# Sixty 64-column zero matmuls in place of two 512-column ones ahead of a two-layer convolution and MLP kernel

## The chip, the cores and the metric

The kernel runs on one core of a Trainium2 chip. The metric is the device time in microseconds of one execution, as the median of several runs; lower is better. The engines are called PE or TensorE (matmuls; PEld is its weight load), DVE or VectorE, ACT or ScalarE, POOL or GpSimd, and SP, which here only issues transfers.

## The reference

Two layers, each made of a gated long convolution (A) and an MLP (B), with the same weights in both layers. The sequence has 2048 positions, the width is 512 and the MLP's inner width 1376.

```
def _A_ref(q, k, v, shift_k, ssm_k, ssm_D):        # S = 2048, D = 512
    k_shift = sum over t < 4 of k delayed by t, times shift_k[:, t]
    kv = k_shift * v
    y = irfft(rfft(kv padded to 2S) * rfft(ssm_k padded to 2S))[:S]   # causal long convolution
    return q * (y + kv * ssm_D)
def _B_ref(x, w1, b1, w2, b2):
    return gelu(layernorm(x) @ w1 + b1) @ w2 + b2

x = A_q
x = x + _A_ref(_layernorm(x), A_k, A_v, A_shift_k, A_ssm_k, A_ssm_D)
x = x + _B_ref(_layernorm(x), ...)
x = x + _A_ref(_layernorm(x), ...)
x = x + _B_ref(_layernorm(x), ...)
```

## The kernel before

The convolution's factor y + kv * ssm_D does not depend on x, so it is computed once and used in both layers. Everything lies in one SBUF tensor "ar" (bf16), a small one "sm" (f32) and PSUM "ps", which is handed out in pieces of two banks or one.

Operations are recorded first (`P.op`), with the memory that they read and write; then a list `ORDER`, written out in the file, gives the order of all operations on all engines, `BANKS` gives each PSUM tile its bank, and semaphore waits are worked out from the recorded dependences. Each engine runs its own operations strictly in that order. Loads are issued by SP, a few small ones by ACT, and wait for nothing.

The stages in the order in which they touch the first 65 us:

- L493 (POOL) clears a 128x512 block; L499 (PE) multiplies that block of zeros with itself eight times into the first PSUM tile ("warm"). Nobody reads the result.
- L528 (PE) transposes the filter `ssm_k` in four groups of 16 matmuls, each behind its load; L453 copies each group out (DVE). L450 on POOL and DVE adds `ssm_D` into one row of each group. L511 (PE) spreads the shift taps over all partitions.
- L545 (PE) is the first stage of the filter's transform, 16 operations of 16 matmuls; L453 (ACT or DVE) evicts each one. L558 (PE) is the second stage, 16 operations of 8 matmuls, evicted by L453 as well.
- The shift of k by up to three positions is done in two ways. For channel blocks 0 and 1 PE transposes k (L589) and multiplies it with diagonal matrices of the taps (L606); the eight matrices, 128x128 each, are made by POOL (L520) from the identity, and L613 (DVE) multiplies with v. For channel blocks 2 and 3 DVE does it with elementwise operations of 128x2048 (L450).
- Then the same transform for kv (L545), its second stage (L651), the product with the filter (L450), and two inverse stages (L674, L731), with evictions by L453.

POOL's order in this part is: memsets (L504, L493, L471), L517, two small L450 (each behind a VectorE copy of L528's results), two memsets (L489), four L520, a small memset (L710), four L520. The matrices are made for the blocks in the order 0, 1, 0, 1 and then 0, 1, 1, 0; so the first L606, which is block 1's, needs the seventh, and block 0's needs the eighth.

From about 76 us on, the layers run: layer norm statistics and updates on DVE and POOL (L754 to L768, L450), transposes, the MLP's matmuls (L827, L860), the gelu on ACT (L832) and the addition on DVE (L864).

Of the kernel before, what the change touches and what calls it, by code (L numbers as in the profile page):

```python
# [367 lines left out]
def bass_interleave_layers__ssm_conv_h3__mixer_channel_mlp__prompt_kernel(  # L368
# [7 lines left out]
    def A(p0, n, off, *dims):  # L376
        return bass.AP(ar, p0 * AR + off, [[AR, n]] + [list(d) for d in dims])
# [7 lines left out]
    def Q(tile, p0, n, off, *dims):  # L385
        return bass.AP(ps, p0 * 4096 + tile.base * 512 + off, [[4096, n]] + [list(d) for d in dims])
# [65 lines left out]
    def evac(engs, dst, src, tile):  # L452
        f = {ACT: lambda e: e.activation(dst, src(), AF.Copy), DVE: lambda e: e.tensor_copy(dst, src())}  # L453
        return P.op(engs, f, writes=[dst], tile=tile)
# [14 lines left out]
    z = A(0, 1, R_K + c0, [512, 3], [1, WDV])  # L469
# [17 lines left out]
    for i in range(NPE):  # L487
        z = A(0, 128, R_KT[i], [130, 16], [1, 2])
# [3 lines left out]
    z = A(0, 128, R_W, [1, 512])  # L492
    P.op(POOL, lambda e, z=z: e.memset(z, 0.0), writes=[z])  # L493
    P.tag = "warm"
    tl = Tile(2)

    def f(e, tl=tl, z=z):
        for i in range(8):
            r = e.matmul(Q(tl, 0, 128, 0, [1, 512]), z[:, :128], z, start=True, stop=True)  # L499
        return r  # L500
    warm = P.op(PE, f, reads=[z], tile=tl)

    one = A(0, 1, R_ONE, [1, 128])
    P.op(POOL, lambda e: e.memset(one, 1.0), writes=[one])  # L504
    P.tag = "taps"
    tl = Tile(2)
    ins = [(i, A(0, 1, R_SR + 512 * c, [1, 512])) for i, c in enumerate(DV_CH)]

    def f(e, ins=ins, tl=tl):
        for i, m in ins:  # L510
            r = e.matmul(Q(tl, 0, 128, 512 * i, [1, 512]), one, m, start=True, stop=True)  # L511
        return r
    P.op(PE, f, reads=[one] + [m for _, m in ins], tile=tl).preds[warm.i] = "psum"
    for i in range(NDV):
        evac(ACT, A(0, 128, R_SJ + i * 512, [128, 4], [1, 128]), lambda tl=tl, i=i: Q(tl, 0, 128, 512 * i, [1, 4], [4, 128]), tl)
# [6 lines left out]
    for b in range(4):  # L522
        tl = Tile(2)
# [27 lines left out]
    def stage2(G, ks, n):  # L551

        tl = Tile(2)
        ins = [(i, A(0, 128, R_S2 + k * 128, [1, 128]), A(0, 128, G + k * n, [1, n])) for i, k in enumerate(ks)]

        def f(e):
            for i, w, m in ins:
                r = e.matmul(Q(tl, 0, 128, i * n, [1, n]), w, m, start=True, stop=True)  # L558
            return r
        P.op(PE, f, reads=[x for y in ins for x in y[1:]], tile=tl)  # L560
        return tl
# [5 lines left out]
    for k8 in range(16):  # L567
        tl = stage2(R_G, range(8 * k8, 8 * k8 + 8), 128)
# [203 lines left out]
    def ntmp():  # L772
        nn[0] += 1
        return R_N + (nn[0] % 8) * 512
# [3 lines left out]
    for L in range(2):  # L778
        s0 = 0
        for n in (BLOCKS0, BLOCKS1)[L]:  # L780
# [6 lines left out]
            for i, s in enumerate(sl):  # L787
                z = ntmp()
# [12 lines left out]
            for i, s in enumerate(sl):  # L801
                z = ntmp()
# [6 lines left out]
                tl = Tile(1)  # L809
# [9 lines left out]
            for fc in range(11):  # L819
                rows = 128 if fc < 10 else 96  # L820
                tl = Tile(1)
# [13 lines left out]
            for i, s in enumerate(sl):  # L835
                P.tag = "m2"
                tl = Tile(1)
# [63 lines left out]
```

## Time and profile before

| what | value |
|---|---|
| median of 3 runs | 241.46 us (241.1 to 242.47) |
| span of the profiled execution, first to last instruction | 238.8 us (the page gives no other time of that execution) |
| PE busy | 226.2 us (95%), 2312 matmuls |
| PEld busy | 151.6 us (63%) |
| DVE busy | 171.6 us (72%) |
| ACT busy | 138.3 us (58%) |
| POOL busy | 41.3 us (17%) |
| eight warm matmuls (L499) | 1.56 to 4.9 us, 3.33 us busy |
| first filter transpose (L528) | starts at 4.78 us |

All positions are in us from the first instruction of the profiled execution. Busy time is the time in which at least one instruction of an engine is recorded as running; matmuls overlap each other, so the spacing of two starts says more than the duration of one. "issue" stands for time in which an engine waited for nothing that the profile shows. An arrow names what ended an idle time.

### The profile page before, as it was taken

Reading aid. Unit: us, or ns where it says so; the run is one execution under the profiler, and the core shown is the slowest. Engines: PE = TensorE matmul, PEld = TensorE weight load, DVE = VectorE, ACT = ScalarE, POOL = GpSimd, SP = SyncE. Lnnn points to the kernel's source line nnn. Section 1 sums busy time; section 2 is a strip of 40 time slices with the busy share of each in tenths; the row PEclk is TensorE's granted clock in tenths of the full one; section 3 lists DMA queues with packets and bytes.
Section 4 is the critical chain, followed back from the end, with each engine's and each line's share of the span. In section 5 each row is a group of like instructions: output and inputs, shape, how many; then the busy total and the mean of one; then the engine's idle time right before and its main releaser. Section 6 shows DMA issues by size and latency. Waiting matters only on the chain.

```text
span 238.8 us, 5555 instructions
## 1 busy us (share of the span) xinstructions
PE 226.2 (95%) x2312; PEld 151.6 (63%) x2332; DVE 171.6 (72%) x359; ACT 138.3 (58%) x225; POOL 41.3 (17%) x77
## 2 busy tenths in 40 slices
PE   7987989886999999999999999999999999999995
PEld 3875778875899886766766667644444444444543
DVE  0979999999999999999887999693793312030035
ACT  2598799999999995642754444342782042454100
POOL 2179000000013444041230310400220200000000
PEclk9999999999999999999999999999999999999999
DMA  6999949999960003111122022240013021310024
GB/s 241 364 342 383 383 148 253 249 272 309 379 227 0 3 0 68 26 23 31 37 47 44 0 48 44 45 88 3 0 22 66 3 44 31 101 44 3 0 71 148
DMA packets 37035, 27.40 MB, mean 115 GB/s; under 512 B 19506, under 2 KB 29969, under 8 KB 37010
## 3 DMA queue, kind: packets, MB, share of 16 engines
q1 hardware_dynamic: 36446, 26.91, 37.8%
q8 instruction: 18, 0.29, 0.5%
q10 hardware_dynamic: 564, 0.14, 0.4%
q14 instruction: 7, 0.06, 0.1%
HBM read 16.82 MB, written 2.10 MB: 79 GB/s over the span
## 4 chain that ended last, share of the span: by engine, by line
PE 77%; ACT 9%; DMA 4%; DVE 4%; SPq 3%; issue 3%; ACTq 0%
PE ps L860 31%; PE ps L827 30%; ACT ar L453 9%; PE ps L674 5%; PE ps L731 3%; SPq L439 3%; PE ps L545 3%; DMA ar<-in_A_ssm_k_dram 2%; DVE ar L453 2%; DMA ar<-ar 2%; PE ps L528 1%; PE ps L606 1%; PE ps L849 1%; DVE sm L754 1%; PE ps L589 1%
## 5 line engine op out<-in xcount | busy, mean ns | idle before, releaser
L832 ACT ACTIVATE ar<-ps,sm 128x256 bf16<-128x256 f32 (+4 forms) x143 | 64.7, 525 | 72.5 <-PE ps L827 68.1
L827 PE MATMUL ps<-ar 128*128 128x256 bf16 (+4 forms) x568 | 84.2, 297 | 0.2
L860 PE MATMUL ps<-ar 128*128 128x512 bf16 (+1 forms) x329 | 79.0, 379 | 0.6
L453 ACT ACTIVATE ar<-ps 128x1024 bf16<-128x1024 f32 (+1 forms) x81 | 72.5, 1057 | 9.0 <-PE ps L511 4.5
L827 PEld LDWEIGHTS ps<-ar 128*128 128x128 bf16 (+1 forms) x572 | 52.9, 100 | 29.8 <-ACT ar L832 0.5
L450 DVE TENSOR_TENSOR ar<-ar 128x512 bf16<-128x512 bf16 (+3 forms) x106 | 63.6, 634 | 2.0 <-DMA ar<-in_A_k_dram 1.3
L860 PEld LDWEIGHTS ps<-ar 128*128 128x128 bf16 (+1 forms) x341 | 33.1, 98 | 34.3 <-ACT ar L832 0.3
L864 DVE TENSOR_TENSOR ar<-ar,ps 128x512 bf16<-128x512 bf16 x31 | 20.6, 680 | 47.3 <-PE ps L860 47.3
L754 DVE BATCH_NORM_STATS2 sm<-ar 128x6 f32<-128x512 bf16 (+1 forms) x68 | 42.8, 647 | 0.1
L768 DVE TENSOR_SCALAR ar<-ar,sm 128x512 bf16<-128x512 bf16 x64 | 25.0, 407 | 7.8 <-POOL sm L762 5.2
L760 POOL TENSOR_SCALAR sm<-sm 128x2 f32<-128x2 f32 (+2 forms) x26 | 6.0, 232 | 93.9 <-DVE sm L756 93.3
L762 POOL TENSOR_TENSOR sm<-sm 128x2 f32<-128x2 f32 (+2 forms) x26 | 21.6, 832 | 2.2
L545 PE MATMUL ps<-ar 128*64 128x128 bf16 x512 | 17.1, 221 | 1.4 <-issue 0.8
L545 PEld LDWEIGHTS ps<-ar 128*64 128x64 bf16 x512 | 14.9, 110 | 3.2 <-issue 1.0
L674 PE MATMUL ps<-ar 128*128 128x128 bf16 x256 | 15.0, 220 | 0.6 <-ACT ar L453 0.6
L674 PEld LDWEIGHTS ps<-ar 128*128 128x128 bf16 x256 | 14.7, 114 | 0.8 <-ACT ar L453 0.8
L453 DVE CAST ar<-ps 128x1024 bf16<-128x1024 f32 x11 | 13.0, 1212 | 0.3 <-PE ps L558 0.3
L651 PE MATMUL ps<-ar 128*128 128x64 bf16 x256 | 9.8, 194 | 3.2 <-ACT ar L453 2.7
L453 DVE COPY ar<-ps 128x2048 bf16<-128x2048 bf16 (+1 forms) x8 | 8.2, 1024 | 6.4 <-PE ps L528 6.3
L651 PEld LDWEIGHTS ps<-ar 128*128 128x128 bf16 x256 | 8.2, 98 | 4.7 <-ACT ar L453 3.9
L756 DVE BATCH_NORM_AGGREGATE sm<-sm 128x2 f32<-128x6 f32 (+1 forms) x64 | 9.9, 171 | 0.3
L558 PE MATMUL ps<-ar 128*128 128x128 bf16 x128 | 8.6, 220 | 0.8 <-ACT ar L453 0.8
(34 smaller groups left out, 78.1 us busy)
## 6 DMA issues: line engine op xcount, KB each, us to landing
ar<-tab_s SPq DMA_DIRECT2D x16, 256.0 KB, 9.6
ar<-ar SPq DMA_DIRECT2D x16, 256.0 KB, 4.2
ar<-in_A_ssm_k_dram SPq DMA_DIRECT2D x4, 512.0 KB, 5.3
ar<-in_A_k_dram SPq DMA_DIRECT2D x8, 256.0 KB, 7.6
ar<-in_A_v_dram SPq DMA_DIRECT2D x8, 256.0 KB, 9.6
ar<-in_A_q_dram SPq DMA_DIRECT2D x4, 512.0 KB, 7.9
out_dram<-ar SPq DMA_DIRECT2D x7, 256.0 KB, 2.1
ar<-in_B_w_dram SPq DMA_DIRECT2D x1, 1376.0 KB, 12.6
```

What stands on the lines that cost most here:

```text
L450: return P.op(eng, lambda e: e.tensor_tensor(o, a, b, op), reads=[a, b] + list(more), writes=[o])
L453: f = {ACT: lambda e: e.activation(dst, src(), AF.Copy), DVE: lambda e: e.tensor_copy(dst, src())}
L545: r = e.matmul(Q(tl, 64 * ri, 64, i * 128, [1, 128]), w, m, start=True, stop=True)
L651: r = e.matmul(Q(tl, 0, 128, i * pitch, [1, n]), w, m, start=True, stop=True)
L674: r = e.matmul(Q(tl, 0, 128, i * 128, [1, 128]), w, m, start=q == 0, stop=q == 1)
L754: P.op(DVE, lambda e, sj=sj, x=x: e.bn_stats(sj, x), reads=[x], writes=[sj])
L762: P.op(POOL, lambda e: e.tensor_tensor(r, v, hf, ALU.pow), reads=[v, hf], writes=[r])
L768: P.op(DVE, lambda e: e.tensor_scalar(o, x, m, r, ALU.subtract, ALU.mult), reads=[x, m, r], writes=[o])
L827: r = e.matmul(Q(tl, 0, rows, 0, [1, w]), a, m, start=dk == 0, stop=dk == 3)
L832: P.op(ACT, lambda e, dst=dst, tl=tl, rows=rows, bias=bias, w=w: e.activation(dst, Q(tl, 0, rows, 0, [1, w]), AF.Gelu_apprx_tanh, bias=bia ...
L860: r = e.matmul(Q(tl, 0, 128, 0, [1, 512]), ins[fc][0], ins[fc][1], start=fc == 0, stop=fc == 10)
L864: P.op(DVE, lambda e, x=x, tl=tl: e.tensor_tensor(x, x, Q(tl, 0, 128, 0, [1, 512]), ALU.add), reads=[x], writes=[x], tile=tl)
```

## The change

In the warm operation the eight matmuls of 512 columns become six of 512 columns followed by sixty of 64 columns. All of them use the same zero block, the first 128 columns of it as weights, and write the same PSUM tile. The operation stays one operation of the list, with the same place, the same dependences and the same PSUM tile; all other operations, their order, their engines and their waits are the same in both kernels. Each matmul is issued as a weight load and a matmul, so TensorE's program grows from 16 to 132 instructions here. In the changed kernel, lines behind the change have numbers higher by two.

```
     def f(e, tl=tl, z=z):
-        for i in range(8):
+        for i in range(6):
             r = e.matmul(Q(tl, 0, 128, 0, [1, 512]), z[:, :128], z, start=True, stop=True)
+        for i in range(60):
+            r = e.matmul(Q(tl, 0, 128, 0, [1, 64]), z[:, :128], z[:, :64], start=True, stop=True)
         return r
     warm = P.op(PE, f, reads=[z], tile=tl)
```

## The prediction

> **What bounds the kernel now.** I read the chain of work that ended last first, because the change sits in the first 5 us and only what the chain carries on from there can reach the end. These are its pieces up to 26 us (start, us, what):
>
> ```profile
> 1.18 4.84 DMA ar<-in_A_ssm_k_dram
> ...
> 14.81 0.79 issue
> 15.60 1.47 PE ps L545 x45
> ...
> 20.77 1.31 issue
> 22.08 1.01 PE ps L589 x15
> ...
> 25.32 4.69 ACT ar L453 x5
> ```
>
> The filter (L528, L545) starts behind a load. Twice TensorE stands still for "issue", with no wait on anything in the program. From 25.32 on, ScalarE's evictions set the pace. The waits of ScalarE from 25.3 to 64 us hold one line only (us in total, times, longest):
>
> ```profile
> ACT ar L453 <- PE ps L558: 2.6, 1, 2.6
> ```
>
> The busy times by stretch (PE, PEld, DVE, ACT and POOL busy) say the same:
>
> ```profile
> 25.30:40.00 14.70, 13.50 (x191) 11.06 (x191) 14.55 (x13) 14.68 (x16) 0.00 (x0) 1.00 0.82 247
> 52.00:63.00 11.00, 8.70 (x191) 7.75 (x192) 11.00 (x11) 11.00 (x14) 0.00 (x0) 1.00 0.98 317
> 76.40:121.00 44.60, 44.34 (x381) 33.06 (x385) 42.85 (x132) 27.95 (x68) 15.21 (x33) 1.00 0.14 27
> ```
>
> ScalarE has no gap after 25.32 until 78 us, and from 64 us TensorE is full too (12.85 of 13.40, 44.34 of 44.60). So whatever moves ScalarE's start at 25.32 moves the end by as much. What sets that start is the first tap matmul (L606, 22.88) and the first L558 behind it (24.62). The timeline, engine by engine:
>
> ```profile
> 1.56 3.33 PE L499 MATMUL ps<-ar 128*128 128x512 bf16 x8 [1.56 <-POOL ar L493]
> 4.78 1.22 PE L528 MATMUL ps<-ar 128*128 128x128 bf16 x16
> ...
> 16.42 2.36 DVE L450 TENSOR_TENSOR ar<-ar 128x2048 bf16<-128x2048 bf16 x2 [1.28 <-DMA ar<-in_A_k_dram]
> 19.83 3.58 DVE L450 TENSOR_TENSOR ar<-ar 128x2048 bf16<-128x2048 bf16 x3
> ...
> 13.86 2.70 POOL L520 TENSOR_SCALAR ar<-ar,sm 128x128 bf16<-128x128 bf16 x4
> 16.81 7.07 POOL L520 TENSOR_SCALAR ar<-ar,sm 128x128 bf16<-128x128 bf16 x4
> ```
>
> GpSimd builds the eight diagonal tap matrices (L520). Four take 0.60 each, then 2.36, 0.60, 2.61 and 1.22: the long ones are those that overlap VectorE's L450 runs at 16.42 and 19.83. The first L606 needs the seventh of them, done at 22.57, 0.3 before it starts.
>
> **Step 1, the start of the filter.** Removed: two 512-column matmuls. The trace starts one every 0.425 us; the seventh starts at 4.094 and the full rate comes at 4.49 (the eighth takes 380 ns, the others 631). Added: sixty of 64 columns with 128x128 weights. The nearest row is L651, the same shape at the full rate: a pair of load and matmul every 29.5 ns. At the low rate no such row exists; 512 columns go from 425 to 216 ns (L860, four in 0.86), a ratio of 1.97, hence 58 ns as an estimate. (The page's PEclk row says 9 from the first slice on and does not show this; the spacing does.) From 4.094, seven run slow (0.40) and 53 at full rate (1.56): they end at 6.06, and L528 starts at 6.1 instead of 4.78, **+1.3**. Bounds: all at the full rate, 5.86, +1.1; all at the low rate, 7.57, +2.8. I take 1.3, since the six matmuls before 4.09 are unchanged. L528's load landed at 4.73, so it hides none of this; the second one's load (6.03) did hold TensorE for 0.3, and this now disappears.
>
> **Step 2, to GpSimd.** L528's results go through four VectorE copies of 1.23 (6.04, 7.34, 9.04, 11.65). The second started 0.06 late behind its load and will now follow the first at once; later ones gain a little more against L545. Adding these I get the fourth copy ending at 13.95 instead of 12.88: **+1.05 to +1.1**. GpSimd's 12.96 (L450) waits for it, and behind that, in its own queue, stand two memsets and all eight L520. So L520 starts at 14.95, not 13.86.
>
> **Step 3, the two "issue" stalls.** Between the resumptions at 15.60 and 22.08 TensorE takes 126 weight loads, 126 matmuls and 4 semaphore waits: 256 instructions. The queue "instruction" of TensorE moved 16 KB at 13.01 and 19.54, each landing 1.1 later, and TensorE went on 1.4 to 1.5 after that. So it waits for its own instructions, in blocks of 256; entering a block starts the next fetch, and 6.5 us pass from one entry (15.60) to the next (22.08). The change adds 58 pairs, 116 instructions, so both block ends move 116 instructions forward in the work: into the L545 that ran at 12.41, and into the one that ran at 18.00. The first is reached at 13.9; its block was entered about 6.1 and comes at 12.5 to 13.0, so there is no stall and TensorE regains 0.8. The second, entered about 12.9, comes at 19.4 to 19.9 and is reached at 18.6: a stall of about 1, but now in front of four L545 and not behind them. Redoing the evictions behind it (0.91 each on ScalarE), L589 ends at 22.4 (before 23.04). By TensorE alone L606 would start at 22.3, **0.6 earlier** than before. The third block would come at 26.6, needed at 28: hidden by ScalarE.
>
> **Step 4, what is late instead.** GpSimd. VectorE's run at 16.42 starts with a load of k, which the change does not touch. Before, four L520 had begun by then. At +1.1 the third begins at 16.35 and the fourth, at 17.05, falls into the run. Giving them the slots that the trace shows (one ends at 19.17, one at 19.87, one at 22.57, one at 23.88), the seventh ends at 23.88 instead of 22.57, and L606 starts at 23.93, **+1.05**. If the delay of step 2 is over 1.16, the third misses 16.42 too: the seventh then ends at 24.6 and L606 starts at 24.63, **+1.75**. These are 0.1 us apart in their cause, and I take the first, as my sum is 1.05 to 1.1. [...]
>
> **The sum.** The profiled execution has a span of 238.8; the page gives no other time of it, and the median of the three runs, 241.46, is 2.66 above (start and end around the span). 238.8 + 1.05 = 239.85, and with 2.66 **242.5**, or +0.43%. No other queue issues anything new.
>
> **Rivals.**
> - *The third tap misses the gap* (above): +1.75, 243.2. For it: a margin of 0.1 us, and the arrival of k can differ as much from run to run. Against: my sum falls short of 1.16.
> - *Not slower*: GpSimd is no gate, because L520 gets through beside VectorE after all (its durations are said to be rough), and the block ends now lie better. Then L606 starts at 22.3, L558 waits only for ScalarE's last eviction of the filter's first stage, at 24.1, and starts at 24.2 instead of 24.62: -0.4, 241.1. It decides if the seventh L520 ends before 22.3. Against: two L520 cannot take 2.4 and 2.6 of themselves where six take 0.6 or 1.2.
> [...]
> - *Another block is late*: a fetch under loads takes longer than 7 us and stalls TensorE beyond ScalarE's reserve, +1.5 to +2.5, about 243.5.
> - *The change does nothing of the kind*: that TensorE waits for the load anyway. It landed at 4.73, so no.
>
> **How the numbers follow.** A measurement of this kernel tells about 0.5% (1.21 us) from no change. Chances: +1.05, 0.42; +1.75, 0.28; not slower, 0.13; low rate, 0.10; another block, 0.07. The second, the fourth and the fifth lie beyond 1.21 us (together 0.45, of which 0.02 may fall back inside). The first is only 0.16 below that, and a third of it, 0.13, may come out above: slower 0.43 + 0.13 = 0.56. Of the not-slower case 0.04 may reach beyond -1.21: faster 0.04, and 0.40 is left for the same. The range takes the first two whole with 0.3 of scatter, the upper part of the not-slower case and most of the late block: 241.2 to 243.9; it leaves the low rate out.
>
> **What would show it.** Right: L528 starts near 6.1; no "issue" stall near 15 and one near 18.6 to 19.8, in L545; L589 ends before 23; the seventh L520 ends at 23.9 or 24.6 with two or three of them long; L606 right behind it; ScalarE idle until 26.4 or 27.1 and dense after. Wrong: if L606 starts before 22.9, or starts late although the seventh L520 is done, or if ScalarE's dense part shows gaps.

## The result, and the profile after

The changed kernel takes 242.74 us (median of 12 runs, 242.19 to 243.34) against 241.4 us for the kernel before (12 runs, 240.84 to 242.61): ratio 1.0049, 95% interval 1.0029 to 1.0070. That is 1.3 us more. The forecast was 242.5, in a range of 241.2 to 243.9, with 0.56 for "slower" and 0.40 for "the same"; the measured 0.49% lies just under the 0.5% that the prediction took as the bound between the two.

The profiled execution has a span of 240.6 us (its own time is 242.39, so 1.8 us lie around the span; over all timed executions on record it is 1.75 to 1.96). The span is 1.8 longer than the one shown of before. Its chain of work that ended last, up to 31 us (start, us, what):

```profile
1.56 2.74 PE ps L499 x6
4.30 1.90 PE ps L501 x60
6.20 2.01 PE ps L530 x32
...
18.57 1.91 issue
20.48 0.48 PE ps L547 x9
20.95 0.02 issue
20.98 3.88 ACT ar L453 x4
24.86 1.75 PE ps L608 x13
26.61 0.46 PE ps L560 x8
27.07 0.02 issue
27.09 3.77 ACT ar L453 x4
```

Line numbers are two higher here (L608 is the L606 of before, L560 the L558, L547 the L545, L591 the L589, L522 the L520, and L530 the L528, which the text calls L528 throughout). The warm matmuls now stand in the chain, where before a load stood. There is one pause for "issue" instead of two; it is longer, and it lies in front of the last evictions of the filter's first stage. ScalarE's dense part starts at 27.09 instead of 25.32, **1.77 later**. One step of the chain is not what it says: the first of L608's 14 matmuls has no record in this trace, and its time is put down as a wait for ScalarE. L608's first weight load started at 24.32, right behind those of L591, and in e9 below L608 ran ahead of the end of the same eviction (24.50 against 24.85). So L608 followed TensorE's own work here. GpSimd and TensorE in the timeline:

```profile
14.86 4.37 POOL L522 TENSOR_SCALAR ar<-ar,sm 128x128 bf16<-128x128 bf16 x4
19.49 5.15 POOL L522 TENSOR_SCALAR ar<-ar,sm 128x128 bf16<-128x128 bf16 x4
...
18.16 0.41 PE L547 MATMUL ps<-ar 128*64 128x128 bf16 x7
20.48 2.34 PE L547 MATMUL ps<-ar 128*64 128x128 bf16 x57 [1.91 <-issue]
22.75 1.89 PE L591 MATMUL ps<-ar 128*128 128x128 bf16 x16
24.85 1.38 PE L608 MATMUL ps<-ar 128*128 128x384 bf16 x9 [0.22 <-ACT ar L453]
```

Sixteen L591 take 1.89 us here; before, sixteen L589 took 1.07 (at 17.00). The windows say why: the third number from the end is the granted clock, 0.50 in one stretch.

```profile
18.10:21.60 3.50, 1.59 (x50) 1.38 (x49) 3.50 (x4) 2.27 (x3) 3.25 (x4) 1.00 1.03 380
21.60:25.00 3.40, 3.18 (x42) 2.95 (x38) 2.20 (x3) 3.25 (x4) 2.85 (x3) 0.50 1.06 382
25.00:28.00 3.00, 2.95 (x37) 2.34 (x36) 2.25 (x3) 0.91 (x1) 0.00 (x0) 1.00 1.04 381
```

(Columns: stretch, its length, busy time and count of PE, PEld, DVE, ACT and POOL, granted clock, DMA share, GB/s.) The clock was at half from 21.57 to 24.98 in this execution, from 1.1 us behind the end of the pause on.

From ScalarE's start on, nothing is gained or lost. Taking each ScalarE operation's start less its start in the execution of before, the lag is 1.77 at 25.4 us, 1.71 at 48, 1.76 at 76, 1.77 at 120, 1.77 at 220, and the spans differ by 1.77.

### The profile page after: what moved, and what is told of

The parts are those of the page before. It is cut to its first block, busy times and chain, and to the rows that moved or that the text cites. A ratio compares the mean times of both kernels' runs of the same rounds, so it can differ in the third digit from the quotient of the medians.

```text
span 240.6 us, 5671 instructions
## 1 busy us (share of the span) xinstructions
PE 228.1 (95%) x2370; PEld 154.5 (64%) x2390; DVE 171.5 (71%) x359; ACT 138.3 (57%) x225; POOL 41.1 (17%) x77
## 4 chain that ended last, share of the span: by engine, by line
PE 78%; ACT 11%; DVE 3%; issue 2%; SPq 2%; DMA 2%; POOL 0%; ACTq 0%; POOLq 0%
PE ps L862 30%; PE ps L829 30%; ACT ar L453 10%; PE ps L676 5%; PE ps L733 3%; SPq L439 2%; PE ps L547 2%; PE ps L530 2%; DMA ar<-ar 2%; DVE ar L453 1%; PE ps L608 1%; PE ps L499 1%; PE ps L851 1%; DVE sm L756 1%; PE ps L560 1%
## 5 line engine op out<-in xcount | busy, mean ns | idle before, releaser
L450 DVE TENSOR_TENSOR ar<-ar 128x512 bf16<-128x512 bf16 (+3 forms) x106 | 63.7, 635 | 1.0 <-ACT ar L453 0.5
L547 PE MATMUL ps<-ar 128*64 128x128 bf16 x512 | 17.3, 224 | 2.3 <-issue 1.9
L547 PEld LDWEIGHTS ps<-ar 128*64 128x64 bf16 x512 | 15.3, 112 | 4.0 <-issue 2.1
L560 PE MATMUL ps<-ar 128*128 128x128 bf16 x128 | 8.6, 220 | 0.8 <-ACT ar L453 0.8
```

What stands on the lines that cost most here:

```text
L450: return P.op(eng, lambda e: e.tensor_tensor(o, a, b, op), reads=[a, b] + list(more), writes=[o])
L547: r = e.matmul(Q(tl, 64 * ri, 64, i * 128, [1, 128]), w, m, start=True, stop=True)
```

## The experiments

My theory, called "gates" below: the extra time is not the sixty matmuls as such. It is set by two things that they shift, where TensorE's blocks of 256 instructions end (in the execution of before it stood still for 0.79 and 1.31 us there), and whether GpSimd's taps get in ahead of VectorE's run at about 16.4 us (0.60 us for an L520 ahead of it, 2.36 for the one beside it). The rivals are "delay alone" (the end moves with the first L528), "number of instructions" and "low clock" (the half rate of the profiled run is the cause). Every kernel was timed in turns with the kernel before on the same chip; in part of the executions of most of these kernels, the one before among them, the mean granted clock is 0.990 to 0.993 and not 1.0 (0.993 in the execution above, whose clock was at half for 3.41 us), so a time alone says little and the traces are read as well. Without the executions in which it fell (a mean granted clock below 0.997) the medians are 241.5 for the kernel before, 242.69 for e1, 244.14 for e2, 240.99 for e3, 241.05 for e4 and 243.12 for e5; the changed kernel's is 242.78.

**e1, instructions without delay.** The 104 extra instructions, with no later start.

```
-        for i in range(8):
-            r = e.matmul(Q(tl, 0, 128, 0, [1, 512]), z[:, :128], z, start=True, stop=True)
+        for i in range(60):
+            r = e.matmul(Q(tl, 0, 128, 0, [1, 64]), z[:, :128], z[:, :64], start=True, stop=True)
```

> Only the sixty 64-column matmuls, no 512-column one: 104 more instructions than before, and no later start (50 at 58 ns up to 4.49 and 10 at 29.5 ns end at 4.8, where before L528 started at 4.78). Gates (my theory: block ends of TensorE's instructions, then GpSimd's taps): the block ends fall 104 instructions earlier in the work; the first block is entered at about 7.7 and comes at about 14.2 but is needed at 13.1, the second comes at 20.7 to 21.2 and is needed at 18.5; L606 starts at 23.4 instead of 22.9 and ScalarE's dense part 0.5 to 1.0 later: +0.5 to +1.0 us on before. Delay alone (the end moves by as much as the first L528): 0. [...]

Measured: 243.52 against 241.62, ratio 1.0072 (1.0039 to 1.0104). L528 started at 5.17 in the trace (its load came late), 0.4 later than in the execution shown of before, and ScalarE's dense part at 27.59, 2.27 later. TensorE's part of it:

```profile
18.37 0.58 PE L545 MATMUL ps<-ar 128*64 128x128 bf16 x13
21.14 2.76 PE L545 MATMUL ps<-ar 128*64 128x128 bf16 x51 [2.19 <-issue]
23.83 1.53 PE L589 MATMUL ps<-ar 128*128 128x128 bf16 x16
25.20 0.98 PE L606 MATMUL ps<-ar 128*128 128x512 bf16 x6
```

Delay alone falls: it expected 0, or 0.4 with the late load of this execution. The pause sits where the block end was expected, and the seventh L520 was long done (20.84), so here TensorE's own instructions hold L606, and not the taps. The block came at 21.14, within the time that I had given it (20.7 to 21.2), but the half rate followed at 21.42 and stretched the work behind the pause. The five timed runs with no fall of the clock have a median of 242.69, some 1.2 above those of the kernel before (241.5), beyond the expectation's upper end. The span of this trace is 3.5 longer than the one of before, and not 2.27: the other 1.3 lie behind the last operation, where the last outputs landed later.

**e2, delay without instructions.** `range(8)` becomes `range(14)`, 512 columns each.

> Fourteen 512-column matmuls: L528 starts at 6.0 as in the changed kernel, with 12 more instructions instead of 116. Gates: both block stalls stay behind about the same work as before and come 1.2 later, the seventh L520 ends at 23.9, L606 starts at 24.0: +1.2 us on before, up to +1.9 if a stall of over 2 us brings the half rate. Delay alone: +1.3. Number of instructions alone (the 116 extra ones are the price, not the start): 0 to +0.2.

Measured: 244.14 against 241.62, ratio 1.0084 (1.0051 to 1.0118), +2.0 us by the ratio, and 2.6 where the clock did not fall. The same delay with 104 instructions fewer costs no less than the change (1.0084 against 1.0049, with intervals that overlap), so the number of instructions alone is not the price. L606 was held by GpSimd, as expected:

```profile
22.63 0.35 PE L545 MATMUL ps<-ar 128*64 128x128 bf16 x5 [1.35 <-issue]
22.92 1.07 PE L589 MATMUL ps<-ar 128*128 128x128 bf16 x16
24.37 1.85 PE L606 MATMUL ps<-ar 128*128 128x512 bf16 x13 [0.39 <-POOL ar L520]
```

ScalarE started 1.44 later. What I had not put in is further down: a block end near 46 us now stalls TensorE beyond ScalarE's reserve (0.74 of idle ScalarE at 47.78, TensorE idle 0.71 for "issue" at 46.94), which makes the lag 2.27, and between 90 and 95 us, where L827 waits 0.44 for a transfer, it grows to 2.89.

**e3, the changed kernel with the taps in another order.** In `ORDER`, operations 56 and 58, and 57 and 61, change places, so that GpSimd makes block 1's four matrices first. All operations are kept.

```
-  ... 91, 24, 56, 78, ... 89, 57, 87, ... 80, 61, 29, 183, 58, 199, ...
+  ... 91, 24, 58, 78, ... 89, 61, 87, ... 80, 57, 29, 183, 56, 199, ...
```

> The changed kernel with GpSimd making the four matrices of channel block 1 before those of block 0, so that the first L606 needs the fourth L520 (19.2) and not the seventh (23.9). Gates: L606 starts as soon as TensorE is there: 22.4 without the half rate, and L558 then waits for ScalarE's last eviction at 24.1 to 24.9: 0 to +0.3 us on before, 0.7 to 1.0 less than the changed kernel. Low clock as the cause in every run: L606 at 24.3 as in the profiled run of the changed kernel, no gain over it. Delay alone: no gain, +1.3 on before.

Measured: 241.01 against 241.62, ratio 0.9970 (0.9940 to 0.9999). The whole cost of the change is gone, though L528 started at 6.58 in this trace and the pause for "issue" is still there:

```profile
20.87 1.81 PE L547 MATMUL ps<-ar 128*64 128x128 bf16 x57 [1.74 <-issue]
22.61 1.07 PE L591 MATMUL ps<-ar 128*128 128x128 bf16 x16
23.52 1.91 PE L608 MATMUL ps<-ar 128*128 128x512 bf16 x14
...
25.90 4.69 ACT L453 ACTIVATE ar<-ps 128x1024 bf16<-128x1024 f32 x5 [0.76 <-PE ps L560]
```

L608 now follows L591 at once. ScalarE starts at 25.90, 0.58 later than in the execution shown of before, and the span is 0.56 longer. What is late there is TensorE itself, behind the pause: from 20.87 on L547, L591, L608 and L560 follow one another without idle time, and the last eviction of the first stage, which L560 also needs, was just in time (25.15). This is the run that shows GpSimd's taps as the cause.

**e4, the kernel before with the same order of taps.**

> The kernel before with the same exchange of GpSimd's taps. Gates: before, L606 started 0.3 after the seventh L520 and waited for TensorE, which had stood still until 22.08: -0.3 to 0 us on before; more (-0.5 to -1) only if the runs that took longer than the profiled one did so because the taps were late. Delay alone and low clock: 0.

Measured: 241.06 against 241.62, ratio 0.9964 (0.9926 to 1.0002): 0.9 us less by the ratio, and 0.4 where the clock did not fall, but the interval touches 1, and its own trace has ScalarE's dense part no earlier than the one shown of before (25.61 against 25.32). A gain would fit late taps in part of the executions of the kernel before, of which e7 is one; it is not shown by this time. With e3 this is the fastest version; the two cannot be told apart, and with this order the sixty matmuls cost nothing that was measured.

**e5, the same delay with half the instructions.** `range(60)` becomes `range(30)`, with 128 columns.

> Six 512-column matmuls and thirty of 128 columns in place of sixty of 64: the same 6.0 for the start of L528, 60 instructions fewer than the changed kernel (56 more than before). Gates: the first block is entered only at about 10.0, behind L545's first wait, and comes at 16.5 where it is needed at 14.5; the second comes at 23 and is needed at 21.5; L606 near 24.9: +2 to +3 us on before, more than the changed kernel although it issues less. Delay alone: as the changed kernel, +1.3. Number of instructions as a price by itself: less than the changed kernel, +0.5 to +0.7.

Measured: 243.12 against 241.63, ratio 1.0036 (1.0002 to 1.0069), +0.9 us by the ratio and 1.6 where the clock did not fall: below what I expected and not distinct from the changed kernel, so inconclusive by its time. Its trace has the two pauses where they were expected and L608 at 25.65, right behind L591, with the seventh L522 done at 22.85; but L528 started at 7.09 in it, and it lies 2.8 above the execution shown of before.

**e6, e8, e9, the changed kernel again.** Three more profiled executions, since the one shown above is one of those with the half rate.

> The changed kernel once more, for the trace of another execution. Gates: again one long issue stall in front of the last four L545 near 18.5 to 20.5, and the seventh L520 at 23.9 or 24.6. If the half rate does not follow the stall this time, L589 ends near 23.7 and L606 follows the seventh L520: the start of ScalarE's dense part is 26.4 to 27.1, 1.05 to 1.75 later than in the profiled run of before. Low clock as the cause: without it the lag vanishes.

> The changed kernel a third time, for an execution without the half rate, as most of its timed runs were. Gates: the last four L545 and L589 are done by about 23.7, the seventh L520 at 23.7 to 24.7, L606 within 0.1 behind it, ScalarE's dense part from 26.4 to 27.2: 1.05 to 1.9 on the profiled run of before, all of it carried to the end. Low clock as the cause: without it L606 starts near 22.4 to 23.7 and the span is that of before.

> The changed kernel a fourth time, as e8: without the half rate L606 follows the seventh L520 (gates) or L589 (low clock, delay).

e6 (span 241.3) has the half rate again, behind the same pause: L591 ends at 25.6 and L608 starts right behind it, with the seventh L522 done at 23.70.

```profile
23.70 1.86 PE L591 MATMUL ps<-ar 128*128 128x128 bf16 x16
```

e8 (span 241.3) and e9 (span 240.4) have the full rate throughout behind that pause, and there GpSimd holds L608: the chain of work that ended last runs through GpSimd's matrices to L608 and ScalarE. First e8, then e9, each with two lines of TensorE and then pieces of that chain:

```profile
22.96 1.07 PE L591 MATMUL ps<-ar 128*128 128x128 bf16 x16
25.40 0.87 PE L608 MATMUL ps<-ar 128*128 128x512 bf16 x5 [1.37 <-POOL ar L522]
...
17.20 2.65 POOL ar L522
...
24.65 0.61 POOL ar L522
...
25.40 1.90 PE ps L608 x14
...
27.78 2.85 ACT ar L453 x3
```

```profile
22.31 1.07 PE L591 MATMUL ps<-ar 128*128 128x128 bf16 x16
24.50 1.74 PE L608 MATMUL ps<-ar 128*128 128x512 bf16 x12 [1.12 <-POOL ar L522]
...
23.14 1.23 POOL ar L522
...
24.50 1.90 PE ps L608 x14
...
26.89 3.77 ACT ar L453 x4
```

In e8 two L522 began before VectorE's run (17.10), the third began 0.10 after it and took 2.64; the seventh ended at 25.25. In e9 three began before it (16.87), and the seventh ended at 24.36. So both cases of step 4 occur, 0.9 us apart, and the lag is 2.46 and 1.57. Low clock as the cause falls: without it the lag stays, and TensorE waits 1.1 to 1.4 us for a matrix of taps.

**e7, the kernel before again.**

> The kernel before once more. Its median lies about 0.8 above its profiled execution, if about 1.8 us lie around the span. Gates: the same two stalls near 14.8 and 20.8 and the seventh L520 near 22.6, and in a slower execution a further stall at a block end, most likely near 42 to 45 us, where in the profiled run the block came just in time (44.9 against 44.8). Delay and low clock say nothing of this.

Span 240.0, 1.1 above the execution shown first. VectorE's run started at 17.07 and four L520 had begun by then, yet the seventh ended at 23.22 and L606 started at 23.34, behind it: +0.43 at ScalarE. The lag grows to 0.76 at the block end near 45 us, as expected, and to 1.13 between 100 and 110 us, where L827 waits for a transfer (at 110.37) and not for a block.

## Why the prediction was right

**What bounds the kernel** was right within 0.02 us: the lag at ScalarE's start is the lag at the end, in all four executions of the changed kernel (1.77, 2.46, 2.46 and 1.57 at 25.4 us; 1.77, 2.44, 2.46 and 1.56 at 220 us).

**Step 1** was right: L528 started at 6.01 (6.1 forecast). My estimate of 58 ns for a 64-column pair at the low rate was a little high: the trace has 53.5, and 29 at the full rate. What differs between executions is when the full rate comes: 4.50, 4.91, 5.42 and 6.50 us in the four profiled executions, with L528 at 6.01, 6.20, 6.42 and 6.92. The point moves by 2.0 us between executions of one kernel; no run shows what sets it.

**Step 2** was right: the fourth copy ended at 13.88 (13.95), the first L522 began at 14.86 (14.95).

**Step 3** was right in place and short in size. No first stall; a second one in front of the last four L545, of 1.91 and not 1. The block's transfer began at 17.95 and TensorE went on at 20.47; I had 19.4 to 19.9. What was short is the entry into the block before: I put it at about 12.9, though the same step has that point reached at 13.9; the trace has 13.70, and 6.8 us later TensorE went on. So L589 did not end at 22.4, nor before 23, which I had named as a sign of being right, but at 23.4 and 24.0 with the full rate (e9, e8), and at 24.6 and 25.6 with the half rate. It cost nothing in e8 and e9, since GpSimd was later still. That the pause belongs to the count of instructions and not to the work is shown by all eleven traces: in each it stands behind the 706th recorded instruction of TensorE (weight loads, matmuls and semaphore waits), in L545 in some kernels and in L589 in others. That the entry into a block starts the next transfer fits both traces: the 16 KB transfers on the instruction queue started 3.0 to 4.5 us behind the entries, before at 13.01, 19.54 and 26.56 for entries at 9.91, 15.60 and 22.08 (counted back from the 706th in steps of 256), and now at 10.84, 17.95 and 24.27 for 7.80, 13.70 and 20.48.

**Step 4** was right as a mechanism: three L522 begin in time, the fourth falls into VectorE's run and takes 2.27, and the seventh ended at 23.94 (23.88). Where GpSimd holds the tap matmul (e2, e7, e8 and e9), ScalarE's dense part starts 2.53 us after the seventh matrix is done. In the first profiled execution of the changed kernel it is 3.15 and in e6 4.08: there the half rate held L608 0.6 and 1.55 longer. That L608 starts late although the seventh matrix is done is a sign that I had named as wrong, and in these two it came; the half rate behind the pause was not in my sum. Of the twelve timed executions one had it, so the median is that of the others. Without it the first one would lie at 1.15 (an estimate: 23.94 + 2.53 - 25.32), against the 1.05 forecast. e3, which takes the wait for GpSimd away, takes the cost away.

**The sum** met 1.3 with 1.05 for two reasons that pull apart. The term that was wrong is the 2.66 us around the span: it is 1.8 (242.39 less 240.6), so the profiled execution of before was a fast one, 240.6 and not 241.46. From that one the four profiled executions lie 1.6 to 2.5 higher, not 1.05, because the full rate came later and the taps with it (e8, e9) or the half rate followed the pause (the first and e6). But a median execution of before is itself about 0.8 above the one shown: e7, which is 1.1 above it, has 0.43 at ScalarE's start, mostly from its own late taps, 0.33 at the block end near 45 us and 0.37 at a wait for a transfer near 110 us. In the changed kernel the block ends lie 116 instructions earlier in the work, and in none of its four profiled executions does the lag grow behind 25 us. 240.9 (the mean of the four spans) less 239.6 (241.4 - 1.8) is the measured 1.3, though two of these four have the half rate and one of the twelve timed ones has. That the two errors nearly cancel is luck: with 1.8 in place of 2.66 the same sum gives 241.65, 1.1 below the measurement.

Of the rivals, the third tap missing the gap is real (e8, one of four). The low rate lasted longer in some executions, but not because of the small matmuls (in e7 the kernel before gets the full rate at 6.51), and it moved L528 by 0.9 at most. No run shows the case that the chance of 0.10 for the low rate stands for, with all sixty matmuls at the low rate and L528 2.8 later: in the four profiled executions the full rate came at 4.50 to 6.50 us, and L528 started at 6.01 to 6.92. "Not slower" falls: GpSimd does not get through beside VectorE (2.27 to 2.65 us for an L520 beside its runs, 0.60 alone).

## What to carry to other kernels

A change ahead of a stage is priced where the delay meets something that does not move with it: here a load that starts VectorE at its own time, beside which GpSimd's queue must fit (2.27 to 2.65 us for an L520 beside VectorE's run, 0.60 alone), and the transfers of TensorE's own instructions (6.3 to 7.2 us from the entry into a block of 256 until the next could be used, in the eleven traces). Count instructions as well as their time: the same delay costs at least as much with few instructions (e2), nearly the same instructions cost without the delay (e1), and the two do not add up. Before taking one profiled execution as the base of a sum, ask whether it is a typical one: the time around the span hardly changes (1.75 to 1.96 us here), so a span that is 2.66 below the median time is that of a fast execution, and its slack is not that of the median.

## What the runs showed of the hardware that was not expected

- The granted clock fell to half behind a pause of TensorE of about 2 us. In the changed kernel's first profiled execution the pause was 1.91 us and the fall came at 21.57, after 17.07 us at the full rate, and lasted 3.41; in e6 a pause of 2.2 us was followed by a fall at 21.97, and in e1 one of 2.19 by a fall at 21.42. In the other eight traces the longest pause for "issue" at this place is 0.78 (e7) to 1.74 us (e3), and their mean granted clock is 1.0. What decides it was not tried by itself.
- In e8 an L522 begun 0.10 us after VectorE's run of two L450 (17.10) took 2.64 us, where such a run takes 2.35 to 2.49 us (the executions shown first of before and of the changed kernel, e2, e3 and e4); in the first profiled execution of the changed kernel one begun 0.1 ahead (16.27 against 16.40) took its 0.60.
- TensorE's instructions came too late in the execution of before, where it used up 256 of them in 5.17 us (15.60 to 20.77) while the DMA engines were full (a share of 1.05, 365 GB/s): 6.5 us passed from the entry into a block (15.60) until the next one could be used (22.08), and 6.3 to 7.2 us between the same two points in the eleven traces.
